# Three weight loads issued one cast sooner, and one input load released by another transfer, in a convolution and GELU kernel

## The chip, the cores and the metric

The kernel runs on one core of one Trainium2 chip. The metric is the time of one execution on the device, in microseconds (us); shown are the median of seven runs and one profiled execution.

## The reference

Two stages follow each other. The first is a causal convolution along the sequence, with 7 taps per head; the taps are a softmax of `weight`. The second is a feed-forward layer with an exact GELU.

```python
def _attn_ref(x, weight):                    # x: 8 x 4096 x 192, weight: 8 x 7
    w = np.exp(weight - np.max(weight, axis=-1, keepdims=True))
    w = w / (np.sum(w, axis=-1, keepdims=True) + 1e-09)
    x_pad = np.concatenate([np.zeros((B, K - 1, D)), x], axis=1)
    idx = np.arange(S)[:, None] + np.arange(K)[None, :]
    x_unf = x_pad[:, idx, :].reshape(B, S, K, H, group)      # group = 192 / 8 = 24
    return np.einsum('hk,bskhg->bshg', w, x_unf).reshape(B, S, D)

def _moe_ref(x, w_in, w_out):                # x: 32768 x 192, w_in: 192 x 2048, w_out: 2048 x 192
    h = x @ w_in
    g = 0.5 * h * (1.0 + erf(h / np.sqrt(2.0)))
    return g @ w_out
```

Inputs and output are float32.

## The kernel before

The 32768 tokens are two halves of 16384, which the kernel carries side by side: the first half in SBUF partitions 0 to 63, the second in 64 to 127. Each half is cut into blocks: six of 256 tokens, then blocks of 512. The 192 channels lie in three planes of 64.

A block n goes through these steps. SP loads its x into `xin` with four transfers (`load`, line 334). DVE transposes it into `xT`, channels in partitions (`trans`, line 496). The convolution is done by DVE with one multiply-add for each tap (`conv`, lines 517 and 524), and gives `xc` in bf16; for blocks 0 and 1 alone TensorE does it (`pconv`, line 685), with diagonal matrices `dg` and a bf16 copy `xTb` of x. That copy is made by ScalarE for block 0 and by GpSimd for block 1 (`cast`, line 226), one instruction for each plane. TensorE multiplies `xc` by W_in (`mm1`, line 739), ScalarE applies the GELU from PSUM into `gT` (line 653), TensorE multiplies `gT` by W_out (`mm2`, line 771, or `mm2_t`, line 800, for the later blocks), and the result is copied to `osb` and stored by SP.

W_in comes in three parts by GpSimd's DMA queue with a conversion to bf16 (`win_in`, line 371), each part for the two halves of the partitions; DVE copies each to the other half (`dup`, line 469). W_out comes in four quarters (`wout_in`, line 404), also by GpSimd's queue and with conversion, each 192 KB in SBUF, with a semaphore `S_WOUT[k]` of its own. A transfer raises its semaphore by 16 when all of it has landed.

The order of the work is written out by hand for each engine; an engine runs its own program in order and waits on semaphores. What bears on the change:

- GpSimd issues W_in's last part in two transfers, `win_in(2, 0)` and `win_in(2, 1)` with `S_WIN[4]`, then W_out's first quarter, then the three casts of block 1 with W_out's other quarters between and after them, then `halo(2)`, a small copy into `xT` that needs block 1's transposes. A cast waits for its plane's transpose (`S_TR`).
- TensorE, in the loop over blocks and slots, does `mm1` of one slot, then for block 0 some pieces of block 1's convolution (`behind`: in slots 2, 3 and 4), then units of `mm2` of the block before (for block 0 its own, from slot 5 on). A convolution piece with the first tap waits for the cast of its plane. Before the first unit that needs a quarter of W_out, TensorE waits for that quarter:

```python
if n < 2 and un[:2] == (0, 0) and un[2] % 4 == 0:
    t.wait_ge(S_WOUT[un[2] // 4], 16)
```

  Quarter 0 is first needed after slot 5 of block 0, quarter 1 after slot 6, quarter 2 after slot 7 and quarter 3 after slot 0 of block 1.
- TensorE's `mm1` of block 2 waits for the last two instructions of DVE's convolution of block 2 (`S_CV`), the very last before the third plane.
- SP loads blocks 0 and 1 at the start, block 2 when `S_WIN[4]` is full, block 3 when W_out's last quarter has landed, and then alternates later loads with stores.

Of the kernel before, what the change touches and what calls it, by code (L numbers as in the profile page):

```python
# [11 lines left out]
def bass_lightweight_conv__then__act_gelu_exact_kernel(  # L12
# [90 lines left out]
    def sem(name):  # L103
        return es.enter_context(nc.semaphore(name))

    def ap(t, off, pat):
        return bass.AP(t, off, pat)

    with es:
# [24 lines left out]
        S_WIN = [sem("S_WIN%d" % i) for i in range(5)]  # L134
        S_WOUT = [sem("S_WOUT%d" % i) for i in range(4)]
# [78 lines left out]
        def part(q):  # L214

            return FQ * (0, 4, 2)[q], [[NP * F, 64], *([[F, NP]] if q < 2 else [[4 * FQ, 2 * NP]]), [1, FQ]]


        def cast(e, n, p):
            e.wait_ge(S_TR, NP * n + p + 1)  # L220
            dst = ap(xTb[PC[n]], p * XB + HX, [[NP * XB, 128], [1, WS[n]]])
            src = ap(xT[n % 2], p * XW + HX, [[NP * XW, 128], [1, WS[n]]])
            if n == 0:
                ins = e.activation(out=dst, in_=src, func=AF.Copy)
            else:
                ins = e.tensor_copy(dst, src)  # L226
            ins.then_inc(S_CAST[PC[n]])

        def trd(n):

            return NP * (n + 1) if n < 2 else 2 * NP + n - 1

        def cvd(n):

            return sum(NCV - 2 * (m in K0) for m in range(n + 1) if m not in PC)
# [58 lines left out]
        def store_half(e, g, h):  # L294
            m = NB - 1
            if h == 0:
                wait_ev(e, m, g)
            else:
                e.wait_ge(S_EVB, g + 1)
            e.dma_start(  # L300
                ap(outt, (h * HALF + OFF[m] + 128 * g) * C, [[C, 128], [1, C]]),
                osb[m % 2][:, (4 * h + g) * C : (4 * h + g + 1) * C],
            ).then_inc(S_OUT[m % 2], 16)
# [22 lines left out]
        def load(e, n, qs=(0, 2, 1, 3), sm=None):  # L326
            mb = WS[n] // 32
            if n >= NX:
                e.wait_ge(S_TR, trd(n - NX))
            for q in qs:  # L330
                off = ((q // 2) * HALF + OFF[n]) * D + DQ * (q % 2)
                dst = [[TB // 32 * DQ, 32], [DQ, mb], [1, DQ]]
                src = [[D, 32], [32 * D, mb], [1, DQ]]
                e.dma_start(  # L334
                    ap(xin[n % NX], 32 * q * (TB // 32 * DQ), dst), ap(xt, off, src)
                ).then_inc(sm or S_XIN[n % NX], 16)

        def store(e, m):
            if m < M0:
                for g in range(NG[m]):  # L340
                    wait_ev(e, m, g)
                    e.dma_start(
                        ap(
                            outt,
                            (OFF[m] + 128 * g) * C,
                            [[C, 128], [HALF * C, 2], [1, C]],
                        ),
                        ap(osb[m % 2], g * C, [[8 * C, 128], [4 * C, 2], [1, C]]),
                    ).then_inc(S_OUT[m % 2], 16)
                return  # L350
            wait_ev(e, m, NP - 1)
            for q in range(4):

                e.dma_start(
                    ap(
                        outt,
                        ((q // 2) * HALF + OFF[m]) * C + (q % 2) * (C // 2),
                        [[C, 32], [32 * C, WS[m] // 32], [1, C // 2]],
                    ),
                    ap(  # L360
                        osb[m % 2],
                        32 * q * 8 * C,
                        [[8 * C, 32], [C // 2, WS[m] // 32], [1, C // 2]],
                    ),
                ).then_inc(S_OUT[m % 2], 16)

        @block.gpsimd
        def _(g):
            def win_in(q, hf, sm):
                c0, pat = part(q)  # L370
                g.dma_start(
                    ap(win, 64 * hf * NP * F + c0, pat), ap(wint, c0 + FQ * hf, pat)
                ).then_inc(sm, 16)

            g.wait_ge(S_MSET, 1)
            for hf in range(2):
                m = idb[64 * hf : 64 * hf + 64, :]
                g.affine_select(
                    out=m,
                    in_=m,  # L380
                    compare_op=ALU.is_equal,
                    fill=0.0,
                    base=0,
                    pattern=[[-1, 64]],
                    channel_multiplier=1,
                ).then_inc(S_IDN)
            g.wait_ge(S_IDN, 2)
            g.memset(wnm[:, :], 0.0).then_inc(S_WNM)
            g.memset(ap(xTb[0], HF, [[NP * XB, 128], [XB, NP], [1, HB]]), 0.0).then_inc(S_HALO)
            g.wait_ge(S_WSB, 16)  # L390
            for q in range(2):
                for hf in range(2):
                    win_in(q, hf, S_WIN[2 if q else hf])
            g.wait_ge(S_PRO, 9)
            g.tensor_tensor(  # L395
                ap(dg, 3 * 64, [[KS * 64, 128], [64, KS - 3], [1, 64]]),
                ap(idb, 0, [[64, 128], [0, KS - 3], [1, 64]]),
                ap(wcol, 3, [[32, 128], [1, KS - 3], [0, 64]]),
                ALU.mult,
            ).then_inc(S_DG)  # L400

            def wout_in(k):
                g0, gs = ((0, 1), (4, 1), (2, 4), (3, 4))[k]
                g.dma_start(
                    ap(wout, 2 * g0 * C, [[NF * C, 128], [2 * gs * C, 2], [1, 2 * C]]),
                    ap(woutt, 256 * g0 * C, [[2 * C, 128], [256 * gs * C, 2], [1, 2 * C]]),
                ).then_inc(S_WOUT[k], 16)

            def halo(n):

                t, tw = (xTb[PC[n]], XB) if n in PC else (xT[n % 2], XW)
                dst = ap(t, HF, [[NP * tw, 128], [tw, NP], [1, HB]])
                if n >= 4:
                    g.wait_ge(S_CV, cvd(n - 2))
                if OFF[n] % SEQ == 0:
                    g.memset(dst, 0.0).then_inc(S_HALO)
                    return
                g.wait_ge(S_TR, trd(n - 1))
                src = ap(
                    xT[(n - 1) % 2], HF + WS[n - 1], [[NP * XW, 128], [XW, NP], [1, HB]]  # L420
                )
                g.tensor_copy(dst, src).then_inc(S_HALO)  # L422

            win_in(2, 0, S_WIN[3])
            halo(1)
            g.wait_ge(S_WIN[1], 16)
            win_in(2, 1, S_WIN[4])
            wout_in(0)
            for p in range(NP):
                cast(g, 1, p)  # L430
                if p > 0:
                    wout_in(p)
            wout_in(3)
            halo(2)
            for n in range(3, NB):
                halo(n)
# [411 lines left out]
        @block.sync  # L848
        def _(sp):
            sp.dma_start(wsb[:, :], ap(wt, 0, [[KS, H], [1, KS]])).then_inc(S_WSB, 16)  # L850
            load(sp, 0, (0, 1))

            sp.wait_ge(S_PRO, 2)
            load(sp, 1)
            sp.wait_ge(S_WIN[4], 16)
            load(sp, 2)
            sp.wait_ge(S_WOUT[3], 16)
            load(sp, 3)
            for n in range(1, NB):
                if n + 3 < NB:  # L860
                    load(sp, n + 3)
                store(sp, n - 1)
            for g in range(NG[NB - 1]):
                store_half(sp, g, 0)
            for s in range(2):
                sp.wait_ge(S_OUT[s], OUTS[NB - 1 if (NB - 1) % 2 == s else NB - 2])
# [28 lines left out]
```

## Time and profile before

| | |
|---|---|
| median of 7 runs | 682.84 us (681.96 to 684.63) |
| the profiled execution | 682.68 us, span 680.9 us |
| TensorE matmul busy | 673.8 us (99%) |
| DVE busy | 527.5 us (77%) |
| ScalarE busy | 537.2 us (79%) |
| GpSimd busy | 33.3 us (5%) |
| granted TensorE clock | 0.999 |
| W_out's four transfers, issue to landing, median | 6.1 us |

The profile shows one execution by the hardware profiler, in us from the start of the span. PE is TensorE's matmuls, PEld its weight loads, ACT is ScalarE, POOL GpSimd, SPq and POOLq the engines' DMA issues. A timeline line gives the start, the duration, engine, source line, operation, output and inputs, the count, and in brackets the idle time before it with what ended it. A line of waits gives the total, the number of times and the longest, in us. Instructions that follow each other are merged in a line, so that its duration is that of the group. A matmul's end is modelled.

### The profile page before, as it was taken

How to read it: one execution, taken by the hardware profiler on the slowest of the kernel's cores; microseconds unless marked ns; L12 is line 12 of the kernel's file. 1: busy time of each engine (PE TensorE's matmuls, PEld its weight loads, DVE VectorE, ACT ScalarE, POOL GpSimd, SP SyncE). 2: the span in 40 equal slices, each digit the busy share in tenths (PEclk: the TensorE clock that was granted, in tenths of full speed). 3: DMA queues.
4: the chain of work that ended last, by engine and by line, in shares of the span. 5: the costliest groups of instructions: out<-in, count | busy, mean ns of one | idle time of the engine just before them, and what ended most of it. 6: DMA issues, size and time to landing. Idle time of an engine off the chain costs nothing.

```text
span 680.9 us, 27122 instructions
## 1 busy us (share of the span) xinstructions
PE 673.8 (99%) x12632; PEld 410.5 (60%) x12632; DVE 527.5 (77%) x609; ACT 537.2 (79%) x550; POOL 33.3 (5%) x56
## 2 busy tenths in 40 slices
PE   8899999999999999999999999999999999999998
PEld 7899655555555555555555555555555555555557
DVE  5789978877779777789777798777897777887511
ACT  7799987787787777787777788777778777778772
POOL 6010000000000000000000000000000000000000
PEclk9999999999999999999999999999999999999999
DMA  9435323224442234442244422344422344310213
GB/s 146 113 84 133 80 61 81 47 65 96 95 95 64 45 82 95 94 88 53 51 96 94 95 71 40 81 95 95 96 49 53 90 95 94 83 38 25 49 49 95
DMA packets 134177, 53.66 MB, mean 79 GB/s; under 512 B 127408, under 2 KB 134064, under 8 KB 134064
## 3 DMA queue, kind: packets, MB, share of 16 engines
q1 hardware_dynamic: 130224, 49.76, 32.7%
q0 software_dynamic: 2720, 1.57, 1.8%
q8 instruction: 99, 1.62, 1.0%
q10 hardware_dynamic: 1120, 0.59, 0.3%
q14 instruction: 14, 0.11, 0.1%
HBM read 28.31 MB, written 25.17 MB: 79 GB/s over the span
## 4 chain that ended last, share of the span: by engine, by line
PE 97%; DMA 2%; DVE 0%; SPq 0%; issue 0%; POOL 0%; ACT 0%; ACTq 0%
PE hp L739 48%; PE ob L800 43%; PE ob L771 5%; DMA wout<-in_moe_w_out_dram 1%; PE hp L771 1%; DMA xin<-in_x_dram 1%; DVE xT L496 0%; DMA wsb<-in_weight_dram 0%; SPq L334 0%; DVE win L469 0%; POOL xTb L226 0%; DVE osb L290 0%; ACT wex L589 0%; DVE wrc L448 0%; DVE wmx L442 0%
## 5 line engine op out<-in xcount | busy, mean ns | idle before, releaser
L653 ACT ACTIVATE gT<-hp 128x1024 bf16<-128x1024 f32 x512 | 523.3, 1024 | 130.1 <-PE hp L739 126.4
L739 PE MATMUL hp<-xc,win 64*64 64x512 bf16 (+2 forms) x6072 | 418.9, 365 | 0.7 <-ACT gT L653 0.4
L800 PE MATMUL ob<-gT,wout 64*64 64x512 bf16 x5376 | 366.3, 376 | 0.0
L524 DVE SCALAR_TENSOR_TENSOR acc<-xT,wcol,acc 128x1024 f32<-128x1024 f32 (+1 forms) x330 | 296.3, 956 | 2.8 <-ACT acc L626 2.7
L739 PEld LDWEIGHTS hp<-xc,win 64*64 64x64 bf16 (+1 forms) x6072 | 188.0, 106 | 134.1 <-ACT gT L653 0.9
L800 PEld LDWEIGHTS ob<-gT,wout 64*64 64x64 bf16 x5376 | 172.2, 118 | 122.9
L321 DVE STREAM_TRANSPOSE osb<-ob 128x512 f32<-128x512 f32 x84 | 74.7, 892 | 128.5 <-PE ob L800 128.5
L496 DVE STREAM_TRANSPOSE xT<-xin 128x1536 f32<-128x1536 f32 (+2 forms) x39 | 75.2, 1933 | 6.3 <-DMA xin<-in_x_dram 6.2
L524 DVE SCALAR_TENSOR_TENSOR xc<-xT,wcol,acc 128x1024 bf16<-128x1024 f32 (+1 forms) x66 | 60.7, 962 | 0.0
L771 PE MATMUL ob<-wout,gT 64*128 64x192 bf16 x896 | 47.6, 243 | 1.9 <-DMA wout<-in_moe_w_out_dram 1.7
L422 POOL COPY xT<-xT 128x18 f32<-128x18 f32 x30 | 23.0, 765 | 514.3 <-DVE xT L496 491.9
L771 PEld LDWEIGHTS ob<-wout,gT 64*128 64x128 bf16 x896 | 38.5, 94 | 8.1 <-DMA wout<-in_moe_w_out_dram 2.3
L517 DVE TENSOR_SCALAR acc<-xT,wcol 128x512 f32<-128x512 f32 (+2 forms) x60 | 33.7, 604 | 1.1
L292 ACT ACTIVATE osb<-ob 128x192 f32<-128x192 f32 x2 | 0.7, 332 | 7.1 <-PE ob L771 7.1
L771 PE MATMUL hp<-wout,gT 64*128 64x192 bf16 x128 | 5.9, 243 | 0.0
L290 DVE COPY osb<-ob 128x192 f32<-128x192 f32 x2 | 0.7, 358 | 6.1 <-PE ob L771 6.1
L626 ACT ACTIVATE acc<-xT,wcol 128x256 f32<-128x256 f32 (+1 forms) x9 | 5.2, 579 | 0.2 <-DVE xT L496 0.2
L771 PEld LDWEIGHTS hp<-wout,gT 64*128 64x128 bf16 x128 | 5.3, 94 | 0.0
L667 PE MATMUL hp<-const-bfloat16-1.0 128*128 128x128 bf16 x48 | 4.5, 282 | 0.8 <-PEq L880 0.8
L277 ACT ACTIVATE osb<-ob 128x384 f32<-128x384 f32 x10 | 4.9, 485 | 0.0
L667 PEld LDWEIGHTS hp<-const-bfloat16-1.0 128*128 128x128 bf16 x48 | 4.3, 134 | 0.8 <-issue 0.8
L685 PE MATMUL ob<-xTb,dg 64*64 64x256 bf16 (+1 forms) x112 | 3.9, 246 | 0.7 <-POOL dg L395 0.6
(35 smaller groups left out, 30.1 us busy)
## 6 DMA issues: line engine op xcount, KB each, us to landing
out_dram<-osb SPq DMA_DIRECT2D x124, 192.0 KB, 3.2
xin<-in_x_dram SPq DMA_DIRECT2D x116, 192.0 KB, 4.1
xin<-in_x_dram SPq DMA_DIRECT2D x22, 96.0 KB, 3.2
wout<-in_moe_w_out_dram POOLq DMA_DIRECT2D x4, 192.0 KB, 6.1
win<-in_moe_w_in_dram POOLq DMA_DIRECT2D x4, 96.0 KB, 4.6
win<-in_moe_w_in_dram POOLq DMA_DIRECT2D x2, 192.0 KB, 5.1
out_dram<-osb ACTq DMA_DIRECT2D x4, 96.0 KB, 1.9
out_dram<-osb SPq DMA_DIRECT2D x4, 96.0 KB, 2.4
```

The source lines that it names most:

```text
L277: e.activation(out=dst, in_=src, func=AF.Copy).then_inc(S_EVA)
L321: v.transpose(ap(osb[m % 2], j, [[8 * C, 128], [C // 2, TB // 32], [NP, 32]]), bank(ring(m, j)),).then_inc(S_EV)
L422: g.tensor_copy(dst, src).then_inc(S_HALO)
L496: v.transpose(out, src).then_inc(S_TR)
L517: ins = v.tensor_scalar(a, src, wk, None, ALU.mult)
L524: ins = v.scalar_tensor_tensor(dst, src, wk, a, op0=ALU.mult, op1=ALU.add)
L626: a.activation(out=acc[n % 2][:, p * TB : p * TB + w], in_=ap(xT[n % 2], p * XW + HX, [[NP * XW, 128], [1, w]]), func=AF.Copy, scale=wcol[ ...
L653: a.activation(out=ap(gT[n % 2], i * c * 2 * w, dst), in_=ap(hp[u % 2], 0, src), func=AF.Gelu,).then_inc(S_GELU)
L667: t.matmul(hp[1][:, 0:128], one, one)
L739: ins = t.matmul(hp[u % 2][fo : fo + fw, o : o + w], ap(win, f1, [[NP * F, 64], [2, fw]]), xc[n % 2][r, p * TB : p * TB + w], start=(p == ...
L771: ins = t.matmul(bb[sub], gT[m % 2][r, c0 : c0 + 128], wout[r, CH[sub][i] * C : (CH[sub][i] + 1) * C], start=(ph == 0 and k == 0), stop=(p ...
L800: ins = t.matmul(bank(ring(m, j), slice(64 * h, 64 * h + 64), w), ap(wout, 64 * hf * NF * C + CH[h][i] * C + j, [[NF * C, 64], [NP, 64]],) ...
```

## The change

On GpSimd the second to fourth quarters of W_out are moved up on its queue: the second right behind the first, ahead of block 1's first cast; the third behind the second cast; the fourth, as before, behind the third cast, but without the third quarter ahead of it there. On SP the load of block 2's x waits for W_out's first quarter in place of W_in's last transfer.

```diff
@@ block.gpsimd
             win_in(2, 1, S_WIN[4])
             wout_in(0)
+            wout_in(1)
             for p in range(NP):
                 cast(g, 1, p)
                 if p > 0:
-                    wout_in(p)
-            wout_in(3)
+                    wout_in(p + 1)
             halo(2)
@@ block.sync
             sp.wait_ge(S_PRO, 2)
             load(sp, 1)
-            sp.wait_ge(S_WIN[4], 16)
+            sp.wait_ge(S_WOUT[0], 16)
             load(sp, 2)
             sp.wait_ge(S_WOUT[3], 16)
             load(sp, 3)
```

The order of instructions on GpSimd, from W_out's first quarter on:

```
before: wout 0 | cast 0 | cast 1 | wout 1 | cast 2 | wout 2 | wout 3 | halo 2
after:  wout 0 | wout 1 | cast 0 | cast 1 | wout 2 | cast 2 | wout 3 | halo 2
```

The instructions of the other engines, their number and their order are the same.

## The prediction

> **What bounds the kernel now.** I read the page first: the busy line, then the chain that ended last.
>
> ```profile
> PE 673.8 (99%) x12632; PEld 410.5 (60%) x12632; DVE 527.5 (77%) x609; ACT 537.2 (79%) x550; POOL 33.3 (5%) x56
> PE 97%; DMA 2%; DVE 0%; SPq 0%; issue 0%; POOL 0%; ACT 0%; ACTq 0%
> ```
>
> TensorE is the bound over nearly the whole span of 680.9 us. An edit to the first 20 us can gain only what TensorE idles there, and what it gains or loses stays to the end. So I read next who waited between 14 and 29 us (total us, times, longest), and TensorE's timeline there.
>
> ```profile
> PEld ob L771 <- DMA wout<-in_moe_w_out_dram: 2.3, 2, 2.0
> DVE xT L496 <- DMA xin<-in_x_dram: 5.6, 1, 5.6
> ```
>
> ```profile
> 16.04 0.82 PE L739 MATMUL hp<-xc,win 64*128 64x256 bf16 x12
> 18.60 0.50 PE L771 MATMUL ob<-wout,gT 64*128 64x192 bf16 x8 [1.74 <-DMA wout<-in_moe_w_out_dram]
> 18.94 0.82 PE L739 MATMUL hp<-xc,win 64*128 64x256 bf16 x12
> 19.79 0.91 PE L771 MATMUL ob<-wout,gT 64*128 64x192 bf16 x12
> ```
>
> TensorE starts its last matmul before the wait at 16.59 and gets W_out's third quarter at 18.60; it then waits 0.3 us more for the fourth. All that the earlier quarters can win is 2.0 + 0.3 = 2.3 us. The second limit is DVE: it waits 5.6 us for block 2's x, and then works without a break to block 2's xc:
>
> ```profile
> 27.90 1.14 DVE L524 SCALAR_TENSOR_TENSOR xc<-xT,wcol,acc 128x512 bf16<-128x512 f32 x2
> 29.16 0.82 PE L739 MATMUL hp<-xc,win 64*128 64x256 bf16 x12
> ```
>
> xc is whole at 27.90 + 1.14 = 29.04; TensorE's block 2 starts at 29.16 and asks for the last plane after 4 of 12 matmuls, at about 29.4. Slack about 0.3 us. So TensorE can keep no more than 0.3 us of gain unless block 2's x lands sooner, and if x lands later by d the end moves by d - 0.3.
>
> Next: why are W_out's quarters late? GpSimd issues them so:
>
> ```profile
> 8.61 0.74 POOL L404 DMA_DIRECT2D wout<-in_moe_w_out_dram  x1
> 9.70 0.91 POOL L226 CAST xTb<-xT 128x256 bf16<-128x256 f32 x2 [0.35 <-DVE xT L496]
> 10.56 0.72 POOL L404 DMA_DIRECT2D wout<-in_moe_w_out_dram  x1
> 11.56 0.78 POOL L226 CAST xTb<-xT 128x256 bf16<-128x256 f32 x1 [0.29 <-DVE xT L496]
> 12.29 1.43 POOL L404 DMA_DIRECT2D wout<-in_moe_w_out_dram  x2
> ```
>
> The trace holds sixteen landings for each transfer, one for each DMA engine. For the third quarter (issued 12.29) fifteen lie between 15.54 and 16.43, the last at 18.56; for the fourth (13.00) fourteen by 17.80, the last two at 18.65 and 19.75. One engine is late. It was already late for W_in's last part (fifteen landings by 12.23, the last at 13.67, which releases the x load today), and the trace shows why: two transfers of 16 KB of instructions, from 9.96 to 12.16 and from 15.49 to 17.20. From 12.16 on, the packets of the late engine follow each other without a gap: W_in's part to 13.2, the first quarter to 14.2, the second to 15.2, four packets of the third by 15.49 (60 ns each), the fetch, the other twelve from 17.19 to 18.22, then the fourth quarter to 19.39; landings follow by 0.3 us. From 17.3 to 18.7 single x packets come between, and W_out's pitch is 90 ns instead of 60. When W_out is through, that engine does the rest of x up to 20.29, landed at 20.63. In the DMA view from 18.25 to 19.4 that tail looks like this (q0 is GpSimd's queue, here W_out; q1 is SP's, here x):
>
> ```profile
> DMA  1241112112012012030202020200202020201000
> q1 hardware_dynamic: 84, 0.03, 10.1%
> q0 software_dynamic: 17, 0.01, 6.5%
> ```
>
> The DMA engines are almost idle, while one of them still has 17 W_out packets to move.
>
> **Part 1, W_out's quarters issued one cast sooner.** Removed and added: nothing. GpSimd after: the first quarter's issue ends at 8.61 + 0.74 = 9.35. The second goes at 9.35 instead of 10.56 (1.2 sooner). The first cast starts at 9.35 + 0.72 = 10.07 instead of 9.70; the trace's casts took 0.395, 0.513 and 0.779 us, the longer ones beside DVE's copies of win. With 0.40 to 0.51 each the second cast ends at about 11.05 instead of 10.61. The third quarter then goes at about 11.05 (1.2 sooner). The third cast starts at 11.05 + 0.71 = 11.76 and ends at about 12.5 instead of 12.35, the fourth quarter goes at 12.5 (0.5 sooner), halo(2) behind it at 13.2 instead of 13.69; its reader, DVE's transpose of block 2, comes at 20.65.
>
> What the casts delay: TensorE's convolution of block 1 starts 0.45 later at 10.66, and 0.4 us of that is taken by the hole in front of 12.40, where it waits for the third cast. Left is +0.2 us at 12.5. Convolution copies on DVE, the GELUs and the last win copy move by 0.2 to 0.45 with it, and all of it ends in the wait of 1.97 us from 16.59 to 18.56. Without that cover it would cost 0.2 us; here 0.
>
> What the earlier issue brings: on the fifteen prompt engines up to 1.2 us, which nobody waits for. On the late engine the next quarter's packets are already there whenever it finishes one, so an earlier issue puts nothing sooner: 0. Lower bound: the quarters land as much sooner as they are issued, 18.56 - 1.2 = 17.3 and 19.75 - 0.5 = 19.25, TensorE resumes after the fourth 0.5 us sooner, of which the DVE slack lets 0.3 through unless x gains too. Upper bound: 0, because a queue served in order loses nothing by being filled early. I take 0, by the packets' gapless row.
>
> [...] The row here: the second quarter was issued at 10.557, under a win copy that ran from 10.511 to 10.932, and took 716 ns, against 712 for the one at 12.292. [...]
>
> **Part 2, block 2's x at the first quarter.** SP's queue today:
>
> ```profile
> SPq L334 <- DMA win<-in_moe_w_in_dram: 8.9, 1, 8.9
> SPq L334 <- DMA wout<-in_moe_w_out_dram: 4.2, 1, 4.2
> L334 SPq DMA_DIRECT2D xin<-in_x_dram x26: 311/452/1368, 1.2 to 42.8; - x26
> ```
>
> The first wait ends at 13.69. The first quarter's last landing is at 14.47, on the late engine, unmoved by part 1. So the four x issues move from 13.69-15.49 to 14.49-16.3: 0.8 later. Behind them on SP are only load(3), which waits for the fourth quarter (19.75), and later work. First x packets came 2.5 us after the first issue (16.20), so now at about 17.0. On the late engine x cannot start before the fetch ends at 17.2, now or then; its first x packet was at 17.31. Once there, the x of this engine still ends when everything queued on it ends, 20.29.
>
> Bounds. x lands with its issue, 0.8 later at 21.43: DVE is 0.8 late, TensorE 0.8 - 0.3 = +0.5. Other end: x comes wholly after W_out on the late engine, then ten x packets no longer stretch the third quarter by 30 ns each: 18.26 instead of 18.56, and sixteen in all 0.48 us at the fourth, 19.27; x itself as now; TensorE gains 0.3, which is also what the slack lets through. I take a little gain, -0.1, as x's first packets should come at or just after 17.3.
>
> **Sum.** Part 1 0, part 2 -0.1: the profiled execution took 682.68 us (span 680.9 and 1.8 around it), so 682.6; the median of seven is 682.84, so 682.7.
>
> **Rivals.**
> A. The quarters land as their issue moves (lower bound of part 1). For it: fourteen or fifteen engines do. Against: the gapless late one. x then decides: 682.84 - 0.3 to - 0.5, 682.4.
> B. The instruction fetch is shorter. Other 16 KB fetches of the first 60 us took 0.9 to 1.65 us, those at 9.96 and 15.49 2.2 and 1.7 under W_in's and W_out's traffic, of which more would now be over by 15.5. At 0.9 everything on the late engine, x included, lands 0.8 sooner: 682.0. Were the late engine not hit at all, x and both quarters would land 1.7 sooner and TensorE resume 1.7 sooner: 681.1. It passes 0.2% only with a fetch under 0.3 us.
> C. x lands 0.8 later, upper bound of part 2: 683.3.
> D. Slower: SP's issues collide with the second fetch. The longest x issue (1368 ns, at 22.10) overlaps the next fetch, at 22.14; the usual is 452. Now the third x issue (15.34) and the fourth would meet the fetch at 15.49 to 17.20. Held up to 17.2, the fourth goes 2.2 later than today; if it keeps its 5.6 us from issue to landing, x lands at 22.8, and TensorE loses 2.2 - 0.3 = 1.9: 684.7. Against: 5.6 us is the time behind W_out on the late engine, while the median x load of the start lands in 3.3, which gives 20.5, no loss. It decides from a landing past 20.9, and past 0.2% from 22.3.
>
> **How the numbers follow.** 0.2% is 1.4 us, about what a measurement of this kernel can tell from no change. Forecast 0.58, A 0.11, C 0.10: all within it. B 0.11, of which only part reaches 0.2%, with execution scatter (681.96 to 684.63) helping. D 0.10. Faster 0.13, same 0.75, slower 0.12. The bounds -0.5 and +0.5 give 682.3 to 683.3; with 1 us of scatter for a median on either side the range is 681.3 to 684.2, which leaves B's far end and D out.
>
> **What would show it.** Right: second and third quarters issued near 9.4 and 11, TensorE still held to about 18.3 to 18.6 by W_out, x issued at about 14.5, DVE's block 2 transpose within 0.3 us of 20.65, block 2's matmuls near 29.1. Wrong: no W_out wait; DVE's transpose past 21 with TensorE waiting for DVE near 29; an x issue of over 1 us; a W_out issue far over 0.74.

## The result and the profile after

The changed kernel took 681.03 us (median of 24 executions, 680.47 to 682.46) against 682.28 us for the kernel before, measured beside it (62 executions). The ratio is 0.9977, 95% interval 0.9971 to 0.9984: faster by 0.23%, some 1.5 us (the medians themselves lie 1.25 us apart). The prediction had been 682.7 us with a range from 681.3 and a chance of 0.13 for faster. It was wrong.

The page of the changed kernel, its busy line and its chain:

```profile
span 678.9 us, 27122 instructions
PE 673.8 (99%) x12632; PEld 411.3 (61%) x12632; DVE 527.2 (78%) x609; ACT 537.1 (79%) x550; POOL 32.9 (5%) x56
PE 97%; DMA 2%; POOL 1%; issue 0%; DVE 0%
```

TensorE's work is the same 673.8 us; the span is 2.0 us shorter (680.9 to 678.9). So the gain is idle time of TensorE, and it lies where the prediction had said that it must lie. The waits from 14 to 29 us, and TensorE's timeline there:

```profile
PEld ob L771 <- DMA wout<-in_moe_w_out_dram: 0.6, 1, 0.6
DVE xT L496 <- DMA xin<-in_x_dram: 3.5, 1, 3.5
```

```profile
16.61 0.83 PE L739 MATMUL hp<-xc,win 64*128 64x256 bf16 x12
17.78 0.91 PE L771 MATMUL ob<-wout,gT 64*128 64x192 bf16 x12 [0.33 <-DMA wout<-in_moe_w_out_dram]
18.52 0.82 PE L739 MATMUL hp<-xc,win 64*128 64x256 bf16 x12
```

The wait for W_out's third quarter is gone; the one for the fourth ends at 17.78 instead of 19.79, 2.0 us sooner. GpSimd's timeline shows the cause's first half, the issues:

```profile
8.62 1.47 POOL L404 DMA_DIRECT2D wout<-in_moe_w_out_dram  x2
10.03 0.94 POOL L226 CAST xTb<-xT 128x256 bf16<-128x256 f32 x2
10.92 0.71 POOL L404 DMA_DIRECT2D wout<-in_moe_w_out_dram  x1
11.63 0.62 POOL L226 CAST xTb<-xT 128x256 bf16<-128x256 f32 x1
12.20 0.71 POOL L404 DMA_DIRECT2D wout<-in_moe_w_out_dram  x1
```

They are 1.2, 1.4 and 0.8 us sooner. The landings (last of sixteen, from the trace's records) moved more: first quarter 13.41 (before 14.47), second 14.43 (15.49), third 15.37 (18.56), fourth 17.73 (19.75), block 2's x 18.80 (20.63). The first quarter's 1.1 us is not the change's work: it was issued when it had been (8.62 and 8.61), and in a second profile of the kernel before (e1 below) it landed at 13.13. As it landed sooner, x too was asked for 0.3 us sooner (13.43 instead of 13.69), and x landed 1.8 us sooner. DVE and TensorE follow (a line of DVE's timeline, then one of TensorE's):

```profile
26.06 1.14 DVE L524 SCALAR_TENSOR_TENSOR xc<-xT,wcol,acc 128x512 bf16<-128x512 f32 x2
```

```profile
27.14 0.82 PE L739 MATMUL hp<-xc,win 64*128 64x256 bf16 x12
```

xc of block 2 is whole at 27.20 instead of 29.04, and TensorE starts block 2 at 27.14 instead of 29.16. The gain of W_out's path and that of x's path are nearly equal, 2.0 and 1.8 us; that is why the whole of it stays.

The two profiled executions differ by more than the medians do, and one thing that the median of the kernel before holds has to be told with it: in 36 of its 117 executions whose clock is recorded (those of the comparisons below), TensorE's mean granted clock was 0.995 to 0.998, and they took 684.4 us (683.7 to 686.3); the other 81 took 682.15 us (681.1 to 683.2). Of 36 executions of the changed kernel none had the lower clock; their median is 681.0. So at full clock the change brings 682.15 - 681.0 = 1.15 us, and the rest of the gain is that the half-clock stretch (last section) no longer comes. In the table "full clock" is the median of the executions with a mean clock of 0.9985 or more, and "low" counts the others. The variants were measured in four comparisons, each with the kernel before beside them; its full-clock median was 682.10 in that of e1 to e4, 681.97 in e5 to e8, 682.31 in e9 to e12 and 682.23 in e13 and e14. A variant's gain at full clock is taken below against its own comparison.

| kernel | ratio to before (95%) | full clock, us | low |
|---|---|---|---|
| before | 1 | 682.15 | 36 of 117 |
| changed, again (e4) | 0.9972 (0.9962 to 0.9983) | 680.88 | 0 of 11 |
| part 1 alone (e2) | 0.9986 (0.9977 to 0.9995) | 681.22 | 0 of 11 |
| part 2 alone (e3) | 0.9989 (0.9977 to 1.0000) | 681.87 | 0 of 11 |
| second quarter alone (e6) | 0.9989 (0.9977 to 1.0002) | 681.95 | 1 of 11 |
| third quarter alone (e9) | 0.9982 (0.9971 to 0.9994) | 681.61 | 1 of 11 |
| all quarters at once (e5) | 0.9989 (0.9976 to 1.0002) | 681.81 | 2 of 11 |
| changed, x later (e7) | 0.9972 (0.9958 to 0.9987) | 681.07 | 0 of 11 |
| changed, x much sooner (e8) | 0.9989 (0.9975 to 1.0003) | 681.92 | 1 of 11 |
| changed, no pacing wait (e12) | 0.9982 (0.9973 to 0.9991) | 681.44 | 0 of 11 |
| before, fetch moved (e10) | 1.0007 (0.9993 to 1.0020) | 682.03 | 5 of 11 |
| before, x late (e13) | 1.0011 (0.9993 to 1.0030) | 682.8 | 5 of 11 |
| before, x much sooner (e14) | 0.9976 (0.9961 to 0.9990) | 681.68 | 0 of 11 |
| changed, long wait (e11) | 1.0044 (1.0030 to 1.0058) | none | 6 of 6 |

### The profile page after: what moved, and what is told of

Read it like the earlier page. It is cut to its first block, busy times and chain, and to the rows that moved or that the text cites. A ratio compares the mean times of both kernels' runs of the same rounds, so it can differ in the third digit from the quotient of the medians.

```text
span 678.9 us, 27122 instructions
## 1 busy us (share of the span) xinstructions
PE 673.8 (99%) x12632; PEld 411.3 (61%) x12632; DVE 527.2 (78%) x609; ACT 537.1 (79%) x550; POOL 32.9 (5%) x56
## 3 DMA queue, kind: packets, MB, share of 16 engines
q0 software_dynamic: 2720, 1.57, 1.8%
## 4 chain that ended last, share of the span: by engine, by line
PE 97%; DMA 2%; POOL 1%; issue 0%; DVE 0%
PE hp L739 48%; PE ob L800 43%; PE ob L771 5%; DMA wout<-in_moe_w_out_dram 1%; PE hp L771 1%; DMA win<-in_moe_w_in_dram 1%; POOL wout L404 0%; POOL xTb L226 0%; POOL win L371 0%; DMA wsb<-in_weight_dram 0%; DVE osb L290 0%
```

## The experiments

The first reading of the two profiles was that the instruction fetch differed: in the changed kernel's profile the two 16 KB fetches took 0.96 and 1.29 us, in that of before 2.20 and 1.71. That is the prediction's rival B. So the first four kernels ask whether the change sets the fetch's length (T1), whether it is chance (T2), and which of the two parts brings the gain.

**e1, the kernel before again, no edit.**

> The kernel before once more, unchanged, for a second profile of it. Theory T1 (what is in flight sets the length of the instruction fetch): the first 16 KB fetch after 9 us again takes about 2.2 us, the second about 1.7, W_out's third quarter lands at about 18.5, and TensorE waits some 2.3 us for W_out. Theory T2 (the fetch's length is chance of the execution, and the two profiles happened to differ): the first fetch takes anything from 0.9 to 2.2 us, and W_out's third quarter lands accordingly between 15.4 and 18.6. Time: the same as before, ratio 1.000.

Ratio 1.0005 (0.9992 to 1.0018). The fetches took 0.95 and 0.95 us, not 2.2 and 1.7; yet W_out's third quarter landed at 18.81, as late as ever. So T1 falls in both halves: the length of the fetch is not set by the issue order, and a short fetch does not bring W_out sooner. T2 is right that the length changes from one execution to the next (2.20 and 0.95 us in two profiles of this kernel, 0.95 to 2.2 over all profiles), and wrong that the landings follow it. With W_in in sooner (its last landing at 12.24), x was asked for at 12.26, and its packets came among W_out's. The waits, and the granted clock by stretches (after the busy times of PE, PEld, DVE, ACT and POOL: clock, DMA share, GB/s):

```profile
PEld ob L771 <- DMA wout<-in_moe_w_out_dram: 2.7, 1, 2.7
```

```profile
16.00:18.80 2.80, 0.42 (x8) 0.13 (x4) 0.00 (x0) 1.49 (x2) 0.00 (x0) 0.94 0.91 168
18.80:19.80 1.00, 0.94 (x12) 0.86 (x14) 0.00 (x0) 0.00 (x0) 0.00 (x0) 0.50 0.14 23
19.80:20.80 1.00, 1.00 (x14) 0.71 (x12) 0.24 (x1) 0.00 (x0) 0.00 (x0) 0.50 0.02 7
```

TensorE waited 2.7 us, and worked at half clock afterwards. This is one of the 684 us executions (683.98).

**e2, part 1 alone.**

```diff
-            sp.wait_ge(S_WOUT[0], 16)      # against the changed kernel
+            sp.wait_ge(S_WIN[4], 16)
             load(sp, 2)
```

> Part 1 alone: W_out's quarters issued as in the changed kernel, block 2's x asked for as before. T1: W_out's second quarter is no longer issued during the first fetch, which takes about 1.0 us instead of 2.2; W_out lands at about 15.4 and 17.7 and nearly the whole gain is there, ratio about 0.998. T2: no gain by itself, ratio 1.000 within 0.001, whatever the profile's fetch. T3 (the x load is what stretches W_out, and part 2 is the gain): ratio 1.000, W_out's third quarter near 18.3.

Ratio 0.9986 (0.9977 to 0.9995), 0.9 us at full clock. The first fetch took 1.64 us, and still the third and fourth quarters landed at 15.68 and 17.49, x at 18.60. So the earlier issue works by itself, with a long first fetch too.

```profile
PEld ob L771 <- DMA wout<-in_moe_w_out_dram: 0.5, 1, 0.5
DVE xT L496 <- DMA xin<-in_x_dram: 3.2, 1, 3.2
```

**e3, part 2 alone.**

```diff
-            sp.wait_ge(S_WIN[4], 16)       # against the kernel before
+            sp.wait_ge(S_WOUT[0], 16)
             load(sp, 2)
```

> Part 2 alone: W_out's quarters issued as before, block 2's x asked for when the first quarter has landed. T1: fetches as before (2.2 and 1.7 us), W_out's third quarter 0 to 0.3 us sooner than 18.56, x at 20.6 or up to 0.8 us later: ratio 0.9995 to 1.001. T3: the gain is here, W_out's third quarter at 16 to 17 us, ratio about 0.998.

Ratio 0.9989 (0.9977 to 1.0000); at full clock 0.2 us, and none of 11 executions with the lower clock, where the kernel before has 31%. In its profile (fetches 1.97 and 0.95 us) x was asked for at 14.35; the third quarter landed at 16.45, the fourth at 19.42, x at 20.64:

```profile
PEld ob L771 <- DMA wout<-in_moe_w_out_dram: 1.9, 1, 1.9
DVE xT L496 <- DMA xin<-in_x_dram: 5.6, 1, 5.6
```

T1 had given x's landing right and W_out's wrong; T3 the third quarter right, and the size of the gain too large.

**e4, the changed kernel again, no edit.**

> The changed kernel once more, for a second profile. T1: fetches of about 1.0 and 1.3 us, W_out's third quarter at about 15.4, x for block 2 at about 18.8, ratio 0.9977. T2: other fetch lengths than in the first profile, up to 2.2 us, and W_out's landings with them; the ratio is 0.9977 all the same.

Ratio 0.9972 (0.9962 to 0.9983). Fetches 0.98 and 0.98 us, third quarter at 15.67, fourth at 17.66, x at 18.86: the landings of the first profile within 0.3 us. Within their intervals the two parts add: 0.9986 x 0.9989 = 0.9975.

The DMA traffic gave the next theory, T4. From 13.5 to 14.5 us the DMA view shows, for the kernel before, for e1 and for the changed kernel (q0 is GpSimd's queue, q1 SP's: packets, MB, share of 16 engines):

```profile
q0 software_dynamic: 111, 0.07, 80.0%
```

```profile
q0 software_dynamic: 86, 0.06, 52.8%
q1 hardware_dynamic: 160, 0.06, 30.8%
```

```profile
q0 software_dynamic: 225, 0.16, 115.7%
```

Before, W_out's packets run dry there: 111 and 86 in that microsecond, against 225 (and 228 in e4, 264 in e2). A quarter's first packets landed 3.2 to 3.5 us after its issue in the profile of before (8.61 to 11.96, 10.56 to 13.78, 12.29 to 15.54, 13.00 to 16.51) and never under 3.0 us in the others. A quarter is about 1 us of work for a DMA engine (an estimate from the prediction's rows: 16 packets, 60 ns apart), so issues that start 1.95 and 1.73 us apart, as those of the first three quarters did before, leave a hole. By T4, what isn't moved in the hole is moved later, on all engines. Four kernels test this and x's part (e5 to e8), and e9 the third quarter by itself.

**e5, all quarters in a row, ahead of the casts.**

```diff
             wout_in(1)                     # against the changed kernel
+            wout_in(2)
+            wout_in(3)
             for p in range(NP):
                 cast(g, 1, p)
-                if p > 0:
-                    wout_in(p + 1)
```

> The changed kernel with W_out's quarters all issued in a row, ahead of block 1's casts. T4 (in the kernel before, the DMA engines run out of W_out packets between the quarters, because a quarter's first packets land some 3.2 us after its issue): third quarter issued at about 10.1 and landed at about 14.5, the fourth at about 10.8 and 15.7, no W_out wait of TensorE left; but the casts start 1.5 us later and TensorE's convolution of block 1 with them, so the time is that of the changed kernel or up to 0.7 us more: ratio 0.997 to 0.9985 to the kernel before. T1 (the late engine's queue and the fetch set the landings, not the issue): third and fourth quarter not before 15.3 and 17.3.

Ratio 0.9989 (0.9976 to 1.0002), at full clock 681.81, 0.8 us above the changed kernel. The issues were at 9.29, 9.99 and 10.69; the third quarter landed at 16.40 and the fourth at 17.48, later than T4 had it: in this profile the first fetch took 1.91 us, and from 10.5 to 12 the DMA engines were thin (45 to 79 packets in half a microsecond). The casts started at 11.38, and TensorE stood 1.2 us for them (10.75 to 11.96), where it no longer stood 0.3 us for W_out; the difference is about the loss. So W_out can be issued too early for the work behind it on GpSimd.

**e6, the second quarter alone.**

```diff
             wout_in(0)                     # against the kernel before
+            wout_in(1)
             for p in range(NP):
                 cast(g, 1, p)
-                if p > 0:
+                if p > 1:
                     wout_in(p)
             wout_in(3)
```

> The kernel before with W_out's second quarter alone moved ahead of block 1's casts; third, fourth and x as before. T4: the second quarter lands about 1 us sooner, but the third is issued at 12.3 as before and starts to land at about 15.5, the hole in the DMA traffic moves to 13.5 to 15 us, and the wait for the third quarter stays: ratio 1.000, not under 0.9993. T1 (the second quarter's issue during the first fetch was the cost): first fetch about 1 us and most of the gain of part 1, ratio about 0.9986.

Ratio 0.9989 (0.9977 to 1.0002): not told apart from nothing, and at full clock 681.95 against 681.97 for the kernel before beside it. In the profile (first fetch 1.57 us) the third quarter, issued at 12.24 as before, landed first at 15.52 and last at 17.50, and TensorE waited 1.7 us for W_out; the hole was still there, 78 and 57 packets in the two halves from 13.5 to 14.5.

**e9, the third quarter alone.**

```diff
                 cast(g, 1, p)              # against the kernel before
-                if p > 0:
-                    wout_in(p)
+                if p == 1:
+                    wout_in(1)
+                    wout_in(2)
             wout_in(3)
```

> The kernel before with W_out's third quarter alone moved ahead of block 1's third cast (second, fourth and x about as before). T4 (holes in the DMA traffic from late issues): third quarter issued at about 11.3 instead of 12.3, first landings at about 14.6 instead of 15.5, all landed 0.5 to 1 us sooner; TensorE's wait for it about 1 us shorter: ratio 0.9985 to 0.9995. If only the second quarter's place matters: 1.000.

Ratio 0.9982 (0.9971 to 0.9994), 0.7 us at full clock. Issued at 11.50, the third quarter landed at 14.80 to 16.15, and TensorE no longer waits for it; what is left is the fourth, issued at 12.82 (TensorE's timeline; the edit shifts line numbers by one):

```profile
16.79 0.50 PE L772 MATMUL ob<-wout,gT 64*128 64x192 bf16 x8
17.12 0.82 PE L740 MATMUL hp<-xc,win 64*128 64x256 bf16 x12
18.94 0.50 PE L772 MATMUL ob<-wout,gT 64*128 64x192 bf16 x8 [0.99 <-DMA wout<-in_moe_w_out_dram]
```

T4's half was right here: the landing moves with the issue, and the wait moves to the next quarter.

**e7, the changed kernel with x still later.**

```diff
-            sp.wait_ge(S_WOUT[0], 16)      # against the changed kernel
+            sp.wait_ge(S_WOUT[1], 16)
             load(sp, 2)
```

> The changed kernel with block 2's x asked for when W_out's second quarter has landed, about 1 us later still. T5 (x competes with W_out on the DMA engines): the fourth quarter lands up to 0.3 us sooner than at 17.7, x at about 19.3 instead of 18.8, DVE's xc for block 2 is late by about 0.5 and TensorE loses 0.2 to 0.4 us at block 2: ratio to the kernel before 0.9976 to 0.998. If x doesn't compete: W_out unmoved, the same loss.

Ratio 0.9972 (0.9958 to 0.9987), 681.07: as the changed kernel. In the profile x was asked for at 15.37 and landed at 19.98, and TensorE, ahead of DVE, stood 0.77 us before block 2; W_out's fourth quarter landed at 17.57. That profile's execution took 681.71 us, the longest of the eleven.

**e8, the changed kernel with x much sooner.**

```diff
-            sp.wait_ge(S_WOUT[0], 16)      # against the changed kernel
+            sp.wait_ge(S_WIN[3], 16)
             load(sp, 2)
```

> The changed kernel with block 2's x asked for much sooner, when the first transfer of W_in's last part has landed (about 10.1 us). T5 (x competes with W_out): x's packets run from about 12.5 on, W_out's third and fourth quarter land 0.5 to 1.5 us later than at 15.4 and 17.7, and TensorE's wait for W_out grows by as much, while DVE starts sooner: ratio to the kernel before 0.9985 to 0.9995. If x waits behind the W_out packets already queued: W_out unmoved, x at 18 or sooner, ratio 0.997.

Ratio 0.9989 (0.9975 to 1.0003): most of the gain is given back. x landed at 18.05, the fourth quarter at 19.57, and TensorE waited 1.8 us for it. GpSimd's third cast and with it the fourth quarter's issue (12.95 instead of 12.20) were late here as well, so x's competition need not be all of it. The profile of e11 (below) has the same late issue, 13.01, with x asked for at 13.74, and its fourth quarter landed at 17.97. Here fifteen landings were in by 18.27, and the last lagged with a fetch from 17.20 to 18.33; what of the 1.6 us is x's and what the fetch's stays open.

**e10, the kernel before with the fetch moved.**

```diff
+            few = nc.const_aps.tensor(1.0, (128, 32), BF16)
-            for i in range(48):
+            for i in range(40):
                 t.matmul(hp[1][:, 0:128], one, one)
+            for i in range(32):
+                t.matmul(hp[1][0:32, 0:32], few, few)
```

> The kernel before with 48 more instructions in TensorE's warm-up (40 large and 32 very small matmuls in place of 48 large ones), so that TensorE's program crosses each 256-instruction page 24 matmuls sooner; DMA issues all as before. T6 (the second fetch, at 15.5 to 17.1 us in the kernel before, lands in W_out's tail and keeps one engine's third or fourth quarter back by 1.3 to 2 us): second fetch at about 14 us, third quarter landed by 17.2, TensorE's wait for W_out shorter by about 1 us: ratio 0.9985 to 0.9993. T4 alone (holes): third quarter at 18.4 or so as before, ratio 1.000.

Ratio 1.0007 (0.9993 to 1.0020). The second fetch came at 14.13 and was over at 15.09, before the third quarter's first packet landed (15.77); the third quarter still landed at 18.32. So T6 falls: the fetch at 15.5 is not what keeps W_out back in every execution. x had been asked for at 12.21 here, as in e1.

**e13, the kernel before with x late.**

```diff
-            sp.wait_ge(S_WIN[4], 16)       # against the kernel before
+            sp.wait_ge(S_WOUT[2], 16)
             load(sp, 2)
```

> The kernel before, W_out's issues as before, with block 2's x asked for only when W_out's third quarter has landed. T5 (x's packets keep the third and fourth quarter late): third quarter at about 16.4, fourth at about 17.5, TensorE's wait for W_out under 1 us, no execution with a mean clock under 0.9985; x lands at about 20 to 20.5, so block 2 is about as late as before: ratio 0.998 to 0.9995. T4 alone (issue times): third quarter still at 18 or later, x later than 21, slower than before, ratio 1.001 to 1.003.

Ratio 1.0011 (0.9993 to 1.0030). T4's side came in its numbers (third quarter at 18.25, x at 21.97, the ratio), T5's did not. But a hole alone does not explain the landings: with no x about, fifteen engines had the third quarter by 15.95 and the fourth by 17.33, and one had them at 18.25 and 19.23. In this profile the second fetch ran from 15.45 to 17.11, and the DMA view from 17.2 to 18.25 shows what was left:

```profile
DMA  1001010100101010100101010010010101001010
q0 software_dynamic: 18, 0.01, 8.1%
```

These are packets 60 ns apart with nothing between them, which is read as one engine's row; the records do not name the engine of a packet. With no x about, the fetch is what is left to keep that engine back: it began at 15.45, just after the third quarter's first landing at 15.35. That is read from the order of events.

**e14, the kernel before with x much sooner.**

```diff
-            sp.wait_ge(S_WIN[4], 16)       # against the kernel before
+            sp.wait_ge(S_WIN[3], 16)
             load(sp, 2)
```

> The kernel before, W_out's issues as before, with block 2's x asked for at about 10.1 us. T5: x's packets fill the holes between W_out's quarters and take turns with them; third quarter at 17 to 18.8, fourth at 19 to 20; TensorE waits 1 to 2.7 us for them and some executions show the lower clock: ratio 0.9985 to 1.001. If x does not compete, third quarter at 16.4 as in the run with x asked for late, ratio under 0.9985.

Ratio 0.9976 (0.9961 to 0.9990). At full clock it is 0.55 us; the rest of the ratio is that none of 11 executions had the lower clock, against 9 of 21 of the kernel before beside them. T5 as it was put, that x ahead of W_out costs W_out time, falls: x was asked for at 10.31, its packets ran from 11.76 and filled the holes (413 of them from 12.0 to 13.0, 286 from 14.0 to 14.5), x had landed at 16.29, and the third and fourth quarters landed at 17.17 and 18.12, over a microsecond sooner than before. TensorE's waits became several small ones:

```profile
PEld ob L771 <- DMA wout<-in_moe_w_out_dram: 1.4, 3, 0.8
DVE xT L496 <- DMA xin<-in_x_dram: 1.1, 1, 1.1
```

**e12, the changed kernel without GpSimd's pacing wait.**

```diff
-            g.wait_ge(S_WIN[1], 16)        # against the changed kernel
             win_in(2, 1, S_WIN[4])
```

> The changed kernel without GpSimd's wait for W_in's second transfer ahead of W_in's last one, so that this and all of W_out's quarters are issued up to 1.2 us sooner. T4 (W_out lands as its issue moves, once there are no holes): quarters 3 and 4 at about 14.3 and 16.6, no W_out wait left, block 2's x (asked for at about 12.3) at 17.8; but W_in's first parts and block 1's x share the DMA engines sooner and may come up to 0.5 us later: ratio 0.9962 to 0.998. T1 (the late engine's queue is the limit): W_out's landings as in the changed kernel, ratio 0.9975.

Ratio 0.9982 (0.9973 to 0.9991): no better than the changed kernel, and the ratios do not tell the two apart (0.9 us at full clock here, 1.2 in e4). The fourth quarter landed at 17.14, and TensorE no longer waits for W_out. Instead it has this hole, which waits for nothing that the profile shows:

```profile
12.55 0.84 PE L738 MATMUL hp<-xc,win 64*64 64x256 bf16 x22
14.95 0.30 PE L738 MATMUL hp<-xc,win 64*64 64x256 bf16 x2 [1.55 <-issue]
```

The first instruction fetch started at 12.69, where it starts at 9.3 to 10.1 in the other kernels (8.3 in e10, by its edit), and ended at 13.64; GpSimd's traffic had no gap before it (150 to 185 packets in each half microsecond from 9 to 11), which is read as why it came late and is not shown. Smaller holes at the same two matmuls are in the profiles of before and of e3 (0.4 us at 13.1), whose first fetch ended at 12.2 and 12.0; in e1 and the changed kernel, whose fetch ended at 10.7 and 11.0, there is none. With e7 (0.2 us, fetch ended at 12.04) there are four such holes, and each ended 1.25 to 1.5 us after its fetch. That the hole is TensorE waiting for instructions is read from this order of events, not from a record.

**e11, the changed kernel with a long wait put in.**

```diff
                             t.wait_ge(S_WOUT[un[2] // 4], 16)
+                            if un[2] == 8:
+                                t.wait_ge(S_TR, trd(2))
```

> The changed kernel with TensorE made to wait, ahead of W_out's third quarter, until DVE has transposed block 2 as well (about 20.0 us): a wait of about 3.7 us in place of none there and 0.5 after it. T7 (a wait of TensorE above some 2.5 us, as in the second profile of the kernel before, costs about 3 us at half clock afterwards): granted clock 0.5 for some 3 us after 20 us, time 3.2 + 1.5 us above the changed kernel, about 685.6, ratio to the kernel before 1.005. Without that: 3.2 us above it, about 684.2, ratio 1.0025.

Ratio 1.0044 (1.0030 to 1.0058), 685.66 us, all six executions with the lower clock; 4.7 us above the changed kernel. TensorE stood 3.1 us (17.15 to 20.27), and the clock by stretches shows T7's price:

```profile
20.00:21.00 1.00, 0.72 (x10) 0.76 (x12) 0.96 (x4) 0.00 (x0) 0.20 (x1) 0.50 0.82 194
22.00:23.00 1.00, 1.00 (x12) 0.60 (x8) 1.00 (x3) 0.59 (x1) 0.00 (x0) 0.50 0.77 193
24.00:25.00 1.00, 1.00 (x26) 0.94 (x24) 1.00 (x3) 0.77 (x1) 0.00 (x0) 1.00 0.06 16
```

## Why the prediction was wrong, point by point

- **What bounds the kernel, and the slack of 0.3 us at block 2**: held. The gain is idle time of TensorE before 20 us, and it stayed because x's path gained as much. e7 shows the other side: with x landed at 19.98 TensorE stands before block 2.
- **GpSimd's sequence and the casts**: held. The prediction had the issues at 9.35, 11.05 and 12.5, and they came at 9.33, 10.92 and 12.20. Its line on TensorE's convolution of block 1, "0.45 later at 10.66", does not add up against a start at 10.52 in the profile of before; the first matmuls came at 10.56, and the next, which waited for a cast, at 11.02. No loss shows from the casts' delay. e5 shows the price when the delay is longer than the cover.
- **A W_out issue far over 0.74 us**, one of the signs of a wrong forecast, did not come. The second quarter's issue took 765 ns and the third's 714, where copies of DVE ran beside part of both (9.97 to 10.39 and 11.44 to 11.99); the fourth's, with no copy beside it, took 706.
- **The step that failed**: "On the late engine the next quarter's packets are already there whenever it finishes one, so an earlier issue puts nothing sooner: 0." It made part 1 worth 0. Part 1 alone (e2) measured 0.9 us at full clock, ratio 0.9986, and its quarters landed at 15.68 and 17.49 instead of 18.56 and 19.75. The gapless row was that of one execution, whose first fetch took 2.2 us and left that engine a backlog. In e1 the fetch took 0.95 us and left no backlog to speak of (the last two landings of W_in's last part came at 12.17 and 12.24, where they were at 12.23 and 13.67), and the third quarter landed as late. What the two profiles have in common is the issue times, and with them the hole from 13.5 to 14.5. e2 and e9 show that W_out lands sooner when it is issued sooner. The upper bound of 0 rested on the argument that a queue filled early loses nothing, which no run shows: in e5 the third quarter was issued at 9.99 instead of 10.92 and landed at 16.40 instead of 15.37, in an execution with a longer first fetch.
- **The lower bound of part 1** was not low enough: it had the third and fourth quarters at 17.3 and 19.25, and they landed at 15.37 and 17.73. It also let x stay where it was, since "the x of this engine still ends when everything queued on it ends, 20.29". x landed 1.8 us sooner.
- **Part 2** had been given -0.1 by x's interleaving. Alone it brings 0.2 us at full clock and, in eleven executions, no half-clock stretch. The second was not among the prediction's terms: the trace that it was made from had full clock from 4.24 to 680.08 us, and its 1.97 us wait was taken as the whole price of waiting.
- **The rivals**: A had the mechanism (W_out lands as its issue moves) and a gain held down to 0.3 to 0.5 us by an x that was taken to stay. B had the numbers of the first profile (a first fetch of 0.96 us, everything 1.8 to 2 us sooner) and the wrong cause. C did not come. Of D the first half came: the fourth x issue took 1.64 us beside the fetch at 14.72; but x landed 4.0 us after it, and nothing was lost.

None of the variants beat the changed kernel.

What stays open: what exactly keeps one engine's part of the third quarter back to 18.3 us and later in e1 and e10. In e13 a fetch is left as the cause; in the profile of before a fetch together with a backlog; in e10 no fetch fell into the quarter's landings, in e1 one of 0.95 us, and in both x had been asked for at 12.2. All three are read from the order of events. Over the 16 profiles the last landing of a quarter came more than 1.2 us behind the fifteenth ten times (before, e1, e3, e8, e12, e13), each time with a fetch between that quarter's issue and its last landing; other fetches so placed went with a lag of 0.1 us (third quarter of e2). So an earlier issue may help by closing the hole, or by bringing the third quarter in ahead of the second fetch; e10 speaks against the second as the whole cause, and no run separates the two. That x asked for at 10.3 (e14) or at 14.4 (e3) does better in the old order than at 12.2 to 13.7 is measured, for e3 at the edge of its interval; that it is because x then falls into the hole, or behind the third quarter, is argued only.

## What to carry to other kernels

A queue that looks gapless in one profile may be so by an accident of that execution: before pricing an earlier issue at zero, look whether the traffic of the whole queue has a hole after it, by packets per microsecond, and take a second profile. Transfers with a long time from issue to first landing (3.2 us here) should be issued back to back, as far as the work behind them on the issuing engine has cover. And a wait of TensorE can have a second price: here 3.413 us with 1.96 to 2.79 us of idle time in them were followed by 3.413 us at half clock, and those with 1.54 us or less were not (last section).

## What the runs showed of the hardware

- **The clock.** In each profile with a half-clock stretch (e1, e10, e11, e13) the clock records show full clock for exactly 13.653 us and then half clock (0.50) for 3.413 us; in the profile of before the record of full clock runs from 4.24 to 680.08 us, which is 198 times 3.413 us. This is read as a grid of 3.413 us; by these records it starts at another point of the span in each execution (4.2 us in before, 4.8 in e1, 6.3 in e11). In the grid window ahead of the half clock TensorE's matmuls had been idle 2.05 us (e1), 2.01 (e10), 1.96 (e13) and 2.79 (e11); after windows with 1.54 us (e8) or 1.46 us (e5) of idle time the clock stayed full. The wait of 2.0 us in the profile of before fell on two windows, with 1.03 and 0.81 us of idle time, and kept full clock. The windows of e1, of e8 and the two of before (idle is the length less the first busy time, PE's):

```profile
15.06:18.47 3.41, 1.36 (x28) 0.98 (x22) 0.00 (x0) 2.43 (x3) 0.00 (x0) 1.00 1.03 182
```

```profile
16.23:19.64 3.41, 1.87 (x40) 1.43 (x36) 1.53 (x2) 2.92 (x3) 0.20 (x1) 1.00 0.49 81
```

```profile
14.48:17.89 3.41, 2.38 (x48) 1.91 (x44) 0.58 (x2) 3.33 (x4) 0.00 (x0) 1.00 1.09 199
17.89:21.30 3.41, 2.60 (x48) 1.98 (x50) 0.65 (x1) 1.06 (x2) 0.00 (x0) 1.00 0.25 60
```

By this reading a wait of 2.0 to 2.7 us cost the clock where most of it fell into one window (e1, e10, e13) and not where it fell on two (before). The shortest idle time ahead of the half clock, e13's 1.96 us, is 57% of 3.413 us. Half clock for 3.413 us costs up to 1.7 us (an estimate, half of its length); the executions of the kernel before that had a lower mean clock were 2.2 us longer, and a longer wait in them may be the rest, which is not shown.
- **Instruction fetches.** The trace of before holds 99 instruction transfers of 16 KB on one queue for 12632 matmuls, one for each 128 with their weight loads (255 instructions, put as 256 in what was expected of e10); so they are read as TensorE's program. The first two after 8 us took 0.9 to 2.2 us in the 16 profiles. In e13 one landing of the third quarter came at 18.25, where fifteen were in by 15.95, with a fetch from 15.45 to 17.11; that the DMA engine that brings a piece moves little else meanwhile is the author's reading of this order, and the records do not name the engine. In e12, by the reading there, TensorE stood 1.55 us for a fetch that ended at 13.64.
- **Issues beside a fetch.** In the 16 profiles, between 9 and 25 us, 22 x issues of SP took 0.9 to 1.9 us instead of 0.45 (1.64 in the changed kernel, 0.92 in e12, 1.89 in e1). Each of them ran beside a fetch and ended 0.3 to 0.4 us after the fetch did (16.41 against 16.01 in the changed kernel).
